# The opening of a forward convolution written anew: v and q mirrored on TensorE instead of in DRAM, the filter's fold in PSUM, SyncE's queue in program order

## The chip, the cores and the metric

One core of one Trainium2 chip. The time is that of one launch in microseconds (us), by the device's clock; the median of three runs stands for a kernel.

## The reference

A forward pass of four layers and its backward pass, for 2048 tokens of width 512 in bf16. The gradients of all inputs are outputs too. Only the first layer is touched here:

```python
x = A_q
x = x + _A_ref(_layernorm(x), A_k, A_v, A_shift_k, A_ssm_k, A_ssm_D)   # this layer
x = x + _B_ref(_layernorm(x), B_w1, B_b1, B_w2, B_b2)                  # MLP with gelu
...                                                                    # both once more, shared weights
# _A_ref(q, k, v, shift_k, ssm_k, ssm_D):
k_shift = sum over t < 4 of k_pad[:, t:t + S, :] * shift_k[:, 3 - t]   # a convolution of 4 taps
kv = k_shift * v
y = irfft(rfft(kv, 2 * S) * rfft(ssm_k, 2 * S))[:S]                    # a long convolution
y = y + kv * ssm_D
return q * y
```

## The kernel before

The long convolution is done with matrices. A sequence of 2048 is folded into blocks of 512 (`Fold`), one half of each block taken backwards, so that sums and differences (`fold_x`, then `fold_s` or `fold_d`, then `fold_t`) are multiplied with tables of cosines and sines on TensorE. The 4096-point spectrum is worked through in five groups of frequencies (`GROUPS`; 2, 2, 4, 4 and 4 blocks of 128). The same is done for the filter h (`A_ssm_k`, table `tabN`) and for kv (table `tabF`). `product` multiplies the two spectra per group on VectorE (DVE), `inv_group` transforms back on TensorE (PE), into `W`; `InvBlocks` unfolds on DVE.

Because of the fold, tokens of the second half of each 512 are kept in reversed order. The kernel before makes reversed copies in DRAM for that (`flip_rows`: `vB` of v, `qB` of q, `goB` of the output's gradient), and loads half a slice from the input and half from the copy (`tok_io`). A "slice" is 512 tokens: four slices of k, v, q.

The phase, `phase_conv_forward`, runs so:
- The filter is loaded as `hN`; per chunk of 128 channels PE transposes it (`ha_ps`, `hb_ps`), DVE and ScalarE (ACT) evict to `hA` and `hR`; PE reverses `hR` (`hr_ps` to `hB`), and DVE adds and subtracts (`fold_x<-hA,hB`). `sin_of` makes the tables: DVE computes angles (`tab_u`), ACT takes the sine.
- k is transposed per slice (`k_slice`: `kt_ps`, `kT`), and its convolution with 4 taps is done on PE with diagonal matrices (`ks_slice`: `ks_ps`, evicted by ACT to `ksb`). DVE multiplies with v (`y_res<-ksb,vt`: kv).
- `h_group` makes the filter's spectrum of a group on PE (`sp_ps`), ACT evicts it to `Hg`, and it is stored to `Hspec_d`. Between, PE turns tables (`table_turns`, `tt_ps`).
- kv is folded; `spectrum(g)` makes its spectrum (`KVg`, stored to `KVspec_d`), `load_spec(g)` loads `Hg` back, and then `product`, `inv_group`. q's four slices are normalised (`norm_sums`: statistics, POOL's rstd, `norm_apply`) and stored to `n_d`: slices 2 and 3 ahead of product 0, slices 0 and 1 between products 0 and 2.
- At the end: `x_sl`, the sum of q and the gated convolution, its statistics, and `l_n`, with which the MLP (`phase_mlp`) begins. The MLP first turns its weights on PE (`oo_ps`, evicted by ACT to `w1T_sb` and `w2T_sb`), and 11 one-column matmuls on `l_g` bring the bias b1 into columns.

What sets the order: in this phase the calls on PE and DVE keep the program's order (`Ordered`); the order on SyncE (SP), which issues most DMAs, is set by a scheduler. From the MLP on a planner sets the order; its rows on PE are the same in both kernels.

Of the kernel before, what the change touches and what calls it, by code (L numbers as in the profile page):

```python
# [177 lines left out]
def sin_of(nc, consts, pool, out, krow, pv, shift, np_=P, eng=None):  # L178
    n = krow.shape[-1]
    us = []  # L180
    for c0 in range(0, n, 1024):
        w = min(1024, n - c0)
        u = pool.tile([P, 1024], I32, name="tab_u", tag="tab_u", bufs=3)[0:np_, 0:w]
        (eng or (nc.vector if c0 else nc.gpsimd)).tensor_scalar(out=u, in0=krow[:, c0:c0 + w], scalar1=pv, scalar2=float(shift), op0=ALU.mult, op1=ALU.add)
        us.append((c0, w, u))
    for c0, w, u in reversed(us):
        nc.vector.tensor_single_scalar(out=u, in_=u, scalar=8191, op=ALU.bitwise_and)
        nc.scalar.activation(out=out[:, c0:c0 + w], in_=u, func=ACT.Sin, scale=SIN_SCALE, bias=consts.pibias[0:np_, :])
# [230 lines left out]
def phase_conv_forward(ctx, nc, tc, dims, consts, dram, res, aps):  # L419
# [80 lines left out]

    def ks_slice(i):
        vt = iop.tile([P, 4, D], BF16, name="vt", tag="vt", bufs=2)
        tok_io(nc, vt, v_ap, dram.vB, i)
# [10 lines left out]
        tt(out=kv[:, 4 * i:4 * i + 4, :], in0=ksb, in1=vt, op=ALU.mult)  # L514

    hA = foldp.tile([P, 4, 1024], BF16, name="hA", tag="fold_s", bufs=1)
    hB = foldp.tile([P, 4, 1024], BF16, name="hB", tag="fold_d", bufs=1)
    hR = foldp.tile([P, 4, 1024], BF16, name="hR", tag="fold_t", bufs=2)

    def h_chunk(cc):  # L520
        b = cc * S
        for m in range(2):
            c = slice(m * 512 + cc * P, m * 512 + (cc + 1) * P)
            ps = psum.tile([P, 4, P], F32, name="ha_ps", tag="kt", bufs=2)
            for i in range(4):
                nc.tensor.matmul(ps[:, i, :], lhsT=hN[:, b + 512 * i + m * P:b + 512 * i + m * P + P], rhs=consts.ident,
                                 start=True, stop=True)
            nc.vector.tensor_copy(out=hA[:, :, c], in_=ps)
            ps = psum.tile([P, 4, P], F32, name="hb_ps", tag="ks", bufs=2)
            for i in range(4):  # L530
                t0 = b + 512 * (i or 4) - m * P - P + 1
                nc.tensor.matmul(ps[:, i, :], lhsT=hN[:, t0:t0 + P], rhs=consts.ident, start=True, stop=True)
            nc.scalar.activation(out=hR[:, :, c], in_=ps, func=ACT.Identity)
        ps = psum.tile([4, P], F32, name="hs_ps", tag="kt", bufs=2)
        nc.tensor.matmul(ps, lhsT=hN[:, b + 256:b + S:512], rhs=consts.ident, start=True, stop=True)
        nc.vector.tensor_copy(out=hsp[0:4, cc * P:(cc + 1) * P], in_=ps)

    for cc in range(ND):
        qt, f = cc // 2, cc % 2
        sin_of(nc, consts, gp, tabN[:, f, qt, :], krow, pvn[:, qt:qt + 1], 2048 * (1 - f), eng=nc.vector)  # L540
        h_chunk(cc)
        if cc >= 2:
            k_slice(cc - 2)
    wshf = gp.tile([P, ND, 4], F32, name="wshf")
    nc.vector.tensor_copy(out=wshf, in_=wsh)
    for cc in range(ND):
        for j in range(4):
            nc.vector.tensor_scalar(out=wdiag[:, cc, j, :], in0=consts.ident, scalar1=wshf[:, cc, j:j + 1],
                                    scalar2=None, op0=ALU.mult)

    for m in range(2):
        for i in range(4):
            ps = psum.tile([P, 512], F32, name="hr_ps", tag="ks", bufs=2)
            nc.tensor.matmul(ps, lhsT=consts.anti, rhs=hR[:, i, m * 512:(m + 1) * 512], start=True, stop=True)
# [1324 lines left out]
```

## Time and profile before

| | |
|---|---|
| median of 3 runs | 848.1 us (847.89 to 851.46) |
| profiled execution | 852.29 us, its span 850.5 us |
| mean granted TensorE clock in it | 0.975 of full speed |
| busy: PE, DVE, ACT, POOL | 755.1, 738.5, 576.4, 207.0 us |

A busy time adds the time in which an engine worked on anything; what an engine waits for is seen in the timelines, which give each row's start, its length and, in brackets, the idle time ahead of it with what ended it.

### The profile page before, as it was taken

The numbers are of one execution on the slowest core, as the hardware profiler recorded it, in microseconds if no ns is written. First come the engines' busy times: TensorE is split into PE (matmuls) and PEld (weight loads), VectorE is DVE, ScalarE is ACT, GpSimd is POOL, SyncE is SP. The second block draws the span as 40 slices with busy tenths as digits, with TensorE's granted clock in tenths as the row PEclk, the third lists the DMA queues.
The fourth block names the chain that finished last, engine by engine and source line by source line (L and its number), as shares of the span: only waits on it lengthen the run. The fifth ranks groups of instructions, "written<-read, shape, count | busy, mean of one in ns | idle before, by whom it ended". The sixth has DMA issues, their size and how long they took to land.

```text
span 850.5 us, 13768 instructions
## 1 busy us (share of the span) xinstructions
PE 755.1 (89%) x5065; PEld 451.7 (53%) x5139; DVE 738.5 (87%) x1289; ACT 576.4 (68%) x818; POOL 207.0 (24%) x329
## 2 busy tenths in 40 slices
PE   4787878967988899999999999988999989999996
PEld 3463323445465566567565656633444446856763
DVE  9948479898999999999979998797399989999982
ACT  6867654668999899997779976445333228655662
POOL 5511210020325233333514213240110403400000
PEclk9999998998899899999999999999999999999998
DMA  6588866403644645746867486999699999793311
GB/s 231 206 323 319 290 229 241 156 9 105 185 143 139 165 133 148 210 146 200 201 193 182 135 249 154 292 207 283 185 280 247 200 385 322 249 319 98 106 62 37
DMA packets 203698, 169.40 MB, mean 199 GB/s; under 512 B 94379, under 2 KB 181614, under 8 KB 203374
## 3 DMA queue, kind: packets, MB, share of 16 engines
q1 hardware_dynamic: 187998, 122.07, 51.2%
q0 software_dynamic: 12400, 40.15, 14.0%
q10 hardware_dynamic: 3232, 6.29, 1.9%
q8 instruction: 40, 0.66, 0.3%
q14 instruction: 28, 0.23, 0.1%
HBM read 78.46 MB, written 76.36 MB: 182 GB/s over the span
## 4 chain that ended last, share of the span: by engine, by line
PE 40%; DVE 28%; ACT 17%; issue 6%; DMA 5%; POOL 3%; ACTq 0%; DVEq 0%; POOLq 0%
PE dw_ps L55 12%; ACT l_g L55 8%; DVE l_g L55 7%; PE sp_ps L55 7%; PE mm_ps L55 5%; PE oo_ps L55 5%; PE iv_ps L55 4%; DVE gy_bf L55 4%; PE gh_ps L55 3%; DVE l_h L55 2%; ACT l_n L55 2%; DVE b_junk L55 2%; DVE b1a L55 2%; DMA G<-n_d 2%; DVE ln_sts L55 1%
## 5 line engine op out<-in xcount | busy, mean ns | idle before, releaser
L55 ACT ACTIVATE l_g<-l_g 128x1536 bf16<-128x1536 bf16 (+1 forms) x96 | 134.9, 1439 | 1.0 <-DVE l_g L55 0.8
L55 PEld LDWEIGHTS <-l_h 128*128 128x128 bf16 x704 | 68.9, 98 | 87.5 <-DVE l_h L55 9.2
L55 PEld LDWEIGHTS <-dw_tm 128*128 128x128 bf16 x704 | 66.6, 98 | 74.2 <-issue 5.7
L55 PEld LDWEIGHTS <-w_sb 128*128 128x128 bf16 x836 | 80.3, 100 | 43.7 <-issue 21.9
L55 PE MATMUL mm_ps<-l_nT,w_sb 128*128 128x256 bf16 x704 | 92.4, 278 | 1.2 <-ACT l_g L55 0.4
L55 PE MATMUL oo_ps<-w_sb,l_h 128*128 128x512 bf16 x341 | 82.3, 386 | 7.6 <-DVE l_h L55 6.8
L55 PE MATMUL dw_ps<-G,dw_tm 128*128 128x512 bf16 x340 | 84.4, 382 | 4.2 <-DMA G<-n_d 3.5
L55 PE MATMUL dw_ps<-x_sl,dw_tm 128*128 128x512 bf16 x340 | 83.2, 379 | 1.7 <-ACT dw_tm L1584 1.1
L55 PE MATMUL mm_ps<-l_nT,w2T_sb 128*128 128x256 bf16 x704 | 82.9, 272 | 1.4 <-ACT l_h L55 0.9
L55 PE MATMUL oo_ps<-w1T_sb,l_h 128*128 128x512 bf16 x339 | 77.3, 379 | 1.8 <-DVE l_g L55 0.6
L55 DVE TENSOR_TENSOR l_g<-l_g,l_g 128x1280 bf16<-128x1280 bf16 (+1 forms) x88 | 76.5, 882 | 0.3
L55 PEld LDWEIGHTS <-w2T_sb 128*128 128x128 bf16 x704 | 68.8, 98 | 14.1 <-issue 2.1
L55 ACT ACTIVATE l_h<-mm_ps 128x512 bf16<-128x512 f32 (+1 forms) x96 | 52.1, 598 | 28.0 <-PE mm_ps L55 19.0
L1584 ACT ACTIVATE dw_tm<-dw_tp 128x1024 bf16<-128x1024 bf16 x44 | 44.7, 1024 | 34.5 <-PE dw_tp L55 27.6
L55 DVE TENSOR_REDUCE b1a<-dw_fm 128x1 f32<-128x2048 bf16 x22 | 49.8, 2279 | 3.2 <-DMA dw_fm<-gz_d 3.2
L55 POOL TENSOR_SCALAR l_dg<-ident,b_cols 128x128 bf16<-128x128 bf16 x32 | 31.7, 989 | 75.1 <-DVE b_junk L55 73.7
L55 ACT ACTIVATE l_n<-x_sl,nmr,rstd 128x512 bf16<-128x512 bf16 x48 | 38.2, 857 | 8.2 <-POOL nmr L989 4.6
L1646 ACT ACTIVATE dw_o<-dw_ps 128x512 bf16<-128x512 f32 x22 | 13.1, 597 | 40.2 <-PE dw_ps L55 30.6
L55 POOL TENSOR_SCALAR rstd<-ln_mvs 128x2 f32<-128x2 f32 x20 | 13.3, 664 | 110.1 <-DVE ln_mvs L55 110.0
L55 DVE TENSOR_SCALAR l_g<-l_g 128x1536 bf16<-128x1536 bf16 (+1 forms) x64 | 32.5, 519 | 3.5 <-ACT l_g L55 3.5
L55 ACT ACTIVATE l_g<-mm_ps,b_col 128x256 bf16<-128x256 f32 x77 | 32.9, 539 | 3.6 <-PE mm_ps L55 3.4
L55 PE MATMUL iv_ps<-Yg,tabI 128*128 128x512 bf16 x108 | 26.3, 395 | 8.5 <-DVE Yg L55 8.3
(293 smaller groups left out, 1599.0 us busy)
## 6 DMA issues: line engine op xcount, KB each, us to landing
h_d<-l_h SPq DMA_DIRECT2D x16, 704.0 KB, 4.6
gz_d<-l_h SPq DMA_DIRECT2D x16, 704.0 KB, 4.6
dw_fm<-gz_d SPq DMA_DIRECT2D x22, 512.0 KB, 9.4
l_n<-n_d SPq DMA_DIRECT2D x28, 256.0 KB, 4.7
n_d<-l_n SPq DMA_DIRECT2D x24, 256.0 KB, 2.9
Hspec_d<-Hg ACTq DMA_DIRECT2D x8, 512.0 KB, 3.0
Hg<-Hspec_d SPq DMA_DIRECT2D x3, 1024.0 KB
KVspec_d<-KVg SPq DMA_DIRECT2D x3, 1024.0 KB, 5.2
```

Of the source, the lines that this page charges most:

```text
L55: return self.tc.keep_in_program_order(f(*args, **kwargs))
L1584: nc.scalar.activation(out=dst, in_=ps, func=ACT.Identity)
L1646: nc.scalar.activation(out=o, in_=ps, func=ACT.Identity)
```

## The change

- The tiles of the MLP's weights are allocated first (`weight_tiles`), and serve as landing places for h and then for q. `start_weights` loads the weights themselves after product 0.
- The filter's fold: `h_back` transposes the reversed part to `hR`; `h_both` adds, in PSUM, the transposed chunk and `hR` through a signed, reversed identity (`turn`), for sum and difference at once (`hx_ps`); one eviction per step goes straight to `fold_x`, in turn by ACT and DVE.
- v is loaded in whole slices; PE mirrors two of its four blocks (`vr_ps`), and DVE reads them from PSUM in the product. q is loaded once; PE mirrors it (`q_turn`, `qr_ps`), ACT evicts, POOL stores `qB`. All four slices of q are normalised ahead of product 0, and two of them loaded back from `n_d` into `y_res`.
- `tabN` is built in halves, the second ones after group 1; `h_group(2)` comes ahead of `ks_slice(3)`.
- `vB` and `goB` are made late, after the last KVspec store and ahead of the MLP's first loads.
- SP keeps the program's order too.

The core of the diff (unchanged parts and small rearrangements left out):

```diff
-    nc = Ordered(nc, tc, ("tensor", "vector"))
+    nc = Ordered(nc, tc, ("tensor", "vector", "sync"))
...
-    flip_rows(nc, dram.vB, v_ap, 511)
-    flip_rows(nc, dram.qB, aps["A_q"].flatten_outer_dims(), 511)
...
+    def kv_slice(i):
+        tt(out=kv[:, 4 * i:4 * i + 2, :], in0=ksbs[i][:, 0:2, :], in1=vts[i][:, 0:2, :], op=ALU.mult)
+        for h in (2, 3):
+            ps = psum.tile([P, D], F32, name="vr_ps", tag="kt", bufs=2)
+            nc.tensor.matmul(ps, lhsT=consts.anti, rhs=vts[i][:, 5 - h, :], start=True, stop=True)
+            tt(out=kv[:, 4 * i + h, :], in0=ksbs[i][:, h, :], in1=ps, op=ALU.mult)
...
+    def h_both(cc, m):
+        t, b = hat[cc]
+        ps = psum.tile([P, 2, 4, P], F32, name="hx_ps", tag="sp", bufs=2)
+        for sg in range(2):
             for i in range(4):
+                t0 = b + 512 * i + m * P
+                nc.tensor.matmul(ps[:, sg, i, :], lhsT=t[:, t0:t0 + P], rhs=consts.ident, start=True, stop=False)
+                nc.tensor.matmul(ps[:, sg, i, :], lhsT=turn[:, m, sg, :], rhs=hR[:, 2 * cc + m, i, :], start=False, stop=True)
+        out = hX[:, :, :, m * 512 + cc * P:m * 512 + (cc + 1) * P]
+        if m:
+            nc.scalar.activation(out=out, in_=ps, func=ACT.Identity)
+        else:
+            nc.vector.tensor_copy(out=out, in_=ps)
...
-    for i in range(4):
-        ks_slice(i)
-        if i < 2:
-            h_group(i)
-        if i in (1, 3):
-            sth.append(fh.streams(GROUPS[(i + 3) // 2][0]))
-        tabF_part(i)
+    for s in range(4):
+        nc.sync.dma_start(out=qs[s], in_=tok(aps["A_q"].flatten_outer_dims(), s))
+    k_slice(0)
+    k_slice(1)
+    ks_slice(0)
+    h_group(0)
+    kv_slice(0)
+    load_v(2)
+    k_slice(2)
+    k_slice(3)
+    ks_slice(1)
+    kv_slice(1)
+    load_v(3)
+    h_group(1)
...
+    ks_slice(2)
+    kv_slice(2)
+    sth.append(fh.streams(GROUPS[3][0]))
+    h_group(2, 2)
+    ks_slice(3)
+    kv_slice(3)
...
+    norm_sums(0)
+    h_group(3, 4)
+    norm_sums(1)
+    tabF_part(2)
+    norm_apply(0)
+    norm_apply(1)
+    tabF_part(3)
...
+    sts = [fk.streams(GROUPS[0][0])]
+    norm_sums(2)
+    norm_sums(3)
+    norm_apply(2)
+    norm_apply(3)
...
+    for s in range(2):
+        nc.sync.dma_start(out=ns[s], in_=tok(dram.n[0], s))
...
         if g == 0:
-            norm_sums(0)
-            norm_sums(1)
-            res.w = start_weights(nc, wpool, dims, aps)
-        if g == 1:
-            norm_apply(0)
-            norm_apply(1)
+            start_weights(nc, res.w, dims, aps)
...
+    flip_rows(dram.goB, aps["grad_out"].flatten_outer_dims(), 511, nc.sync)
+    flip_rows(dram.vB, v_ap, 511, nc.sync)
```

Three places in the order of instructions. First DVE behind product 1 (`pr_t`, `pr_u` and `Yg` are a product's steps; `Hg_1307` and `Hg_1457` are the filter's group 1 in the two kernels, `Hg_1496` and `Hg_1547` its group 2). Before:

```order
L55 TENSOR_TENSOR Yg<-pr_u 128x1024
L55 TENSOR_SCALAR fold_s<-fold_d 128x2x1024
L55 TENSOR_SCALAR fold_s<-fold_s 128x1024 x2
L55 TENSOR_TENSOR fold_t<-fold_x,fold_s 128x1024 x2
L55 TENSOR_TENSOR fold_t<-fold_s,fold_x 128x1024 x2
L55 TENSOR_SCALAR y_res<-y_res,rstd_97,ln_nmr 128x512 x8
L55 TENSOR_TENSOR pr_t<-KVg,Hg_1496 128x2048
```

and in the changed kernel:

```order
L55 TENSOR_TENSOR Yg<-pr_u 128x1024
L55 TENSOR_SCALAR fold_s<-fold_d 128x2x1024
L55 TENSOR_SCALAR fold_s<-fold_s 128x1024 x2
L55 TENSOR_TENSOR fold_t<-fold_x,fold_s 128x1024 x2
L55 TENSOR_TENSOR fold_t<-fold_s,fold_x 128x1024 x2
L55 TENSOR_TENSOR pr_t<-KVg,Hg_1547 128x2048
```

The eight applications (`y_res<-y_res,rstd`) ahead of product 2 are gone, as are eight pairs of statistics between products 0 and 1; both now stand before `fold_x` of kv.

Second, SP's queue from group 0's KVspec store to the load of the filter's group 2. Before:

```order
L663 DMA KVspec_d<-KVg 256x1x1024
L246 DMA y_res<-in_A_q_dram 128x2x512
L652 DMA n_d<-y_res 128x4x512
L246 DMA y_res<-qB_d 128x2x512
L652 DMA n_d<-y_res 128x4x512
L246 DMA y_res<-in_A_q_dram 128x2x512
L246 DMA y_res<-qB_d 128x2x512
L657 DMA Hg_1496<-Hspec_d 128x2x2048
```

and in the changed kernel (two `n_d` stores of 128x4x512 and the load of group 1's `Hg`, 128x2x1024, stand right ahead of it):

```order
L55 DMA KVspec_d<-KVg 256x1x1024
L55 DMA y_res<-n_d 128x4x512 x2
L55 DMA w_sb<-in_B_w_dram 128x4x1376
L55 DMA w_sb<-in_B_w_dram 128x10x512
L55 DMA w_sb<-in_B_w_dram 96x512
L55 DMA w_sb<-in_B_b_dram 1x512
L55 DMA KVspec_d<-KVg 256x1x1024
L55 DMA Hg_1547<-Hspec_d 128x2x2048
```

The weights (`w_sb<-in_B_w_dram`), which stood far ahead, behind the loads of v, now stand between group 0's KVspec store and the load of the filter's group 2.

Third, SP's queue at the end of the phase. Before, the last KVspec store is followed at once by the loads of b1 (`l_g<-in_B_b_dram`):

```order
L663 DMA KVspec_d<-KVg 256x1x2048
L55 DMA l_g<-in_B_b_dram 1x4x128
L55 DMA l_g<-in_B_b_dram 1x128
```

and in the changed kernel:

```order
L55 DMA KVspec_d<-KVg 256x1x2048
L55 DMA goB_d<-in_grad_out_dram 1024x1x512
L55 DMA vB_d<-in_A_v_dram 1024x1x512
L55 DMA l_g<-in_B_b_dram 1x4x128
L55 DMA l_g<-in_B_b_dram 1x128
```

Two reversed copies of 1 MB now stand between them; `goB` stood behind the weights before, `vB` at the very start, next to `qB`, which is no longer copied in DRAM.

## Rows read from the trace of the kernel before

**Rows 1.** Timeline of PE, 0 to 66 us: start, length, instruction, idle time before it.
```profile
4.34 0.61 PE L55 MATMUL ha_ps<-ident,hN 128*128 128x128 bf16 x4 [4.34 <-DMA hN<-in_A_ssm_k_dram]
...
39.03 0.38 PE L55 MATMUL sp_ps<-fold_t,tabN 128*128 128x512 bf16 x1 [0.53 <-DVE fold_t L55]
...
56.44 3.73 PE L55 MATMUL ks_ps<-wdiag,kT 128*128 128x128 bf16 x64 [1.10 <-ACT ksb L512]
60.01 0.38 PE L55 MATMUL sp_ps<-fold_d,tabN 128*128 128x512 bf16 x1
...
65.14 1.07 PE L55 MATMUL tt_ps<-ident,tabN 128*128 128x128 bf16 x16
69.31 0.61 PE L55 MATMUL tt_ps<-ident,tabN 128*128 128x128 bf16 x8 [3.10 <-ACT tg L202]
```

**Rows 2.** Timeline of DVE, 9 to 67 us.
```profile
9.20 1.28 DVE L55 CAST hA<-ha_ps 128x512 bf16<-128x512 f32 x2
...
30.90 4.49 DVE L55 TENSOR_TENSOR fold_x<-hA,hB 128x4096 bf16<-128x4096 bf16 x2
35.43 2.29 DVE L55 TENSOR_TENSOR fold_s<-fold_x 128x4096 bf16<-128x4096 bf16 x1
37.75 2.36 DVE L55 TENSOR_TENSOR fold_t<-fold_s 128x2048 bf16<-128x2048 bf16 x2
...
41.52 1.50 DVE L55 TENSOR_SCALAR tab_u<-krow,pvh 128x1024 int32<-128x1024 f32 x2
43.05 1.29 DVE L55 TENSOR_SCALAR tab_u<-tab_u 128x1024 int32<-128x1024 int32 x2
...
62.01 0.16 DVE L55 CAST tabF<-alt 128x1 bf16<-128x1 f32 x1 [5.04 <-ACT tabF L188]
...
65.94 1.22 DVE L55 TENSOR_TENSOR y_res<-ksb,vt 128x2048 bf16<-128x2048 bf16 x1
```

**Rows 3.** Timeline of DVE, 94 to 137 us.
```profile
94.20 1.23 DVE L55 TENSOR_TENSOR fold_t<-fold_s 128x2048 bf16<-128x2048 bf16 x1 [9.11 <-PE sp_ps L55]
...
102.13 1.39 DVE L55 TENSOR_SCALAR y_res<-y_res,rstd,ln_nmr 128x512 bf16<-128x512 bf16 x4 [0.33 <-POOL ln_nmr L989]
...
111.92 1.23 DVE L55 TENSOR_TENSOR pr_t<-KVg,Hg 128x2048 bf16<-128x2048 bf16 x1 [1.77 <-ACT KVg L323]
...
118.27 0.69 DVE L55 BATCH_NORM_STATS2 ln_st<-y_res 128x6 f32<-128x512 bf16 x1
...
125.73 0.47 DVE L55 MEMSET w_sb<- 128x64 uint32 x2
...
133.94 2.67 DVE L55 TENSOR_SCALAR y_res<-y_res,rstd,ln_nmr 128x512 bf16<-128x512 bf16 x8
136.52 1.21 DVE L55 TENSOR_TENSOR pr_t<-KVg,Hg 128x2048 bf16<-128x2048 bf16 x1
```

**Rows 4.** Timeline of SP's queue, 9 to 160 us.
```profile
9.86 0.80 SPq L231 DMA_DIRECT2D vB_d<-in_A_v_dram  x1
...
20.49 12.62 SPq L246 DMA_DIRECT2D vt<-in_A_v_dram  x1
...
157.77 0.52 SPq L663 DMA_DIRECT2D KVspec_d<-KVg  x1
```

**Rows 5.** Table by stretch: length, busy time of PE, PEld, DVE, ACT, POOL, clock, DMA share, GB/s.
```profile
4.00:8.00 4.00, 2.07 (x16) 1.63 (x17) 3.43 (x11) 1.37 (x3) 4.00 (x18) 1.00 1.00 365
...
120.00:124.00 4.00, 4.00 (x20) 1.78 (x19) 2.96 (x8) 2.48 (x3) 1.70 (x4) 1.00 0.97 302
```

**Rows 6.** Timeline of PE, 143 to 178 us.
```profile
143.14 6.63 PE L55 MATMUL iv_ps<-Yg,tabI 128*128 128x512 bf16 x29 [1.70 <-DVE Yg L55]
...
156.52 14.06 PE L55 MATMUL iv_ps<-Yg,tabI 128*128 128x512 bf16 x62
...
177.17 0.42 PE L55 MATMUL oo_ps<-l_g 128*128 128x1 bf16 x11
```

**Rows 7.** Timeline of ACT, from 183 us.
```profile
187.71 2.93 ACT L55 ACTIVATE l_n<-x_sl,nmr,rstd 128x512 bf16<-128x512 bf16 x4 [4.55 <-POOL nmr L989]
```

More of the change, by code (lines that the diff above doesn't have):

```diff
@@ L170, in build_consts @@
         nc.vector.memset(c.pibias, math.pi * (1.0 - SIN_EPS))
+        c.zero = const_pool.tile([P, 1], F32, name="zero")
+        nc.scalar.activation(out=c.zero, in_=c.onescol_f, func=ACT.Sin, scale=0.0)
     return c
@@ L175, with sin_of @@
 SIN_SCALE = -(2.0 * math.pi / 8192.0) * (1.0 - SIN_EPS)
[L178 to L188, printed above, removed]
+def sin_of(nc, consts, pool, out, krow, pv, shift):
+    u = pool.tile([P, 1024], I32, name="tab_u", tag="tab_u", bufs=3)
+    nc.vector.tensor_scalar(out=u, in0=krow, scalar1=pv, scalar2=float(shift), op0=ALU.mult, op1=ALU.add)
+    nc.vector.tensor_single_scalar(out=u, in_=u, scalar=8191, op=ALU.bitwise_and)
+    nc.scalar.activation(out=out(), in_=u, func=ACT.Sin, scale=SIN_SCALE, bias=consts.pibias)
 def table_turns(nc, psum, pool, consts, tabN, dramG, tabF, tabI, dramI):
@@ L207, in table_turns @@
     tgs = {}
-    for f in range(2):
-        for k0 in (0, 8):
+    for k0 in (0, 8):
+        for f in range(2):
             for qt in range(2):
@@ L513, in ks_slice @@
         nc.gpsimd.dma_start(out=dram.ks[:, 4 * i:4 * i + 4, :], in_=ksb)
[L514 to L524, printed above, removed]
-            for i in range(4):
[L526 to L536, printed above, removed]
@@ L538, in phase_conv_forward @@
-    for cc in range(ND):
[L539 to L554, printed above, removed]
-            nc.scalar.activation(out=hB[:, i, m * 512:(m + 1) * 512], in_=ps, func=ACT.Identity)
-    for i in range(2, 4):
-        k_slice(i)
-    krow5 = gp.tile([P, 1024], F32, name="krow5", tag="tab_u", bufs=3)[0:5, 0:5 * P]
-    for gi, (k1, base, n) in enumerate(GROUPS):
-        nc.vector.tensor_copy(out=krow5[:, gi * P:(gi + 1) * P], in_=krow[0:5, base * P:(base + 1) * P])
@@ new lines, in phase_conv_forward, with h_back @@
+    hX = res.xpool.tile([P, 2, 4, 1024], BF16, name="fold_x", tag="fold_x", bufs=1)
+    hR = foldp.tile([P, 8, 4, P], BF16, name="hR", tag="fold_d", bufs=1)
+    def h_back(cc, m):
+        t, b = hat[cc]
+        ps = psum.tile([P, 4, P], F32, name="hb_ps", tag="ks", bufs=2)
+        for i in range(4):
+            t0 = b + 512 * (i or 4) - m * P - P + 1
+            nc.tensor.matmul(ps[:, i, :], lhsT=t[:, t0:t0 + P], rhs=consts.ident, start=True, stop=True)
+        nc.scalar.activation(out=hR[:, 2 * cc + m], in_=ps, func=ACT.Identity)
@@ new lines, in phase_conv_forward @@
+    ps = psum.tile([4, D], F32, name="hs_ps", tag="kt", bufs=2)
+    for cc in range(ND):
+        t, b = hat[cc]
+        nc.tensor.matmul(ps[:, cc * P:(cc + 1) * P], lhsT=t[:, b + 256:b + S:512], rhs=consts.ident, start=True, stop=True)
+    nc.vector.tensor_copy(out=hsp[0:4, :], in_=ps)
+    for f, u in enumerate((sp5u, krow5)):
+        nc.vector.tensor_single_scalar(out=u, in_=u, scalar=8191, op=ALU.bitwise_and)
+        nc.scalar.activation(out=sp5[:, f, :], in_=u, func=ACT.Sin, scale=SIN_SCALE, bias=consts.pibias[0:5, :])
@@ L682, in phase_conv_forward @@
             load_spec(g)
+        if g == 4:
+            res.x = res.xpool.tile([P, NT, D], BF16, name="x_sl", tag="fold_x", bufs=1)
+            for s in range(4):
+                tok_io(nc, res.x[:, s * TS:(s + 1) * TS, :], aps["A_q"].flatten_outer_dims(), dram.qB, s)
         H = Hs[g]
```

216 lines of the change are left out of this document (124 added, 92 removed).

## The prediction, made before the changed kernel was run

> **What bounds the kernel now.** I read the page's busy times first, in the table above: PE is busy 755.1 us of 850.5, DVE 738.5. Neither share says much here, because all edits lie in the forward convolution, before the MLP, and everything from the MLP on is the same work in the same order. So the change is worth the shift of the MLP's start, and I measure that on ACT's first `l_n` (187.71 us, [rows 7]). I then read the start backwards along the timelines.
>
> PE ends the phase with an unbroken run: from Yg's second half of group 2 (143.14) it goes through the last inverse transforms until 170.4 [rows 6]. What lets it start is DVE's product 2 at 136.52, behind product 0 at 111.92 [rows 3]. Between the two DVE has no idle time to speak of: normalising q's first half (statistics 118.27 to 125.73, application 2.67) stands in that stretch. Before product 0 it is PE that holds DVE: the longest wait is 9.11 us, until PE has read the old `fold_t` for the filter's spectrum [rows 3]. In the opening the first spectrum matmul comes at 39.03 [rows 1], behind the filter's fold on DVE (30.90 to 40.1, [rows 2]).
>
> **Part 1, the filter's opening: 13 us earlier.** Removed: the `fold_x` pair of 4.49, the hA casts (8 of 0.64), the reversal through `hr_ps`/`hB`, the krow casts. Added: 8 steps, each 4 + 16 matmuls of 128 columns and an eviction of 1024 from PSUM. A matmul takes 0.0575 us at 56.44 (64 in 3.73) and about 0.105 in the first rows (4 in 0.61, of which some 0.2 is the tail that the next one overlaps) [rows 1]; the granted clock reads 1.00 there too [rows 5], so the rows give two paces and not the reason. A step is then 2.1 us by PE at the slow pace, or 1.35 by DVE's half of the work (a cast of 1024, twice 0.64, and a half table, (1.50 + 1.29)/2, every second step [rows 2]). Eight steps from about 5.5 us (the second part of h) end at 16.5 to 22.5; fold_s 2.3 and fold_t 2.4 follow [rows 2], and waits of about 2. First spectrum matmul at 23 to 29; I take 26, the middle, since the trace gives no rule for when the pace changes. PE has k's first transposes and ks(0) between, 5.6 to 8 by the prices below, which ends at about the same time. 13 us gained.
>
> **Part 2, the gain is spent on PE before the fourth kv product.** PE's new order from there: group 0's 13 matmuls, mirrors, k's transposes of slices 2 and 3, ks(1), group 1, ks(2), then group 2 (40) with 32 turns, and only then ks(3). Prices by [rows 1]: ks 3.73 each, three times, plus up to 0.8 each for evictions; 20 spectrum matmuls 5.13 (60.01 to 65.14), so 10.3 for group 2 and 6.4 for the 25 of groups 0 and 1; 32 transposes of k 1.9 to 3.4 by the two paces; 32 turns 2.1 to 4 (16 in 1.07, then waits for ACT's copies, one of them 3.10); mirrors about 1.3. Sum 33 to 39. I take 38, near the end with the waits, which the rows show on turns. Slice 3's product starts near 64 (56 to 68). Before it was issued at 65.94 [rows 2], so part 1 is gone here: DVE waits for PE in the meantime.
>
> **Part 3, DVE from there to product 0: 3 us later than before.** Its queue, each price a row [rows 2, 3]: kv(3) 1.9; group 4's fold_t 2.4 (as much as the two of 2048); eight half tables 11.2 and two casts 0.3; statistics of q's slices 0 and 1, 6.4 (95.3 to 102.1 less the wait of 0.33); application 2.7; fold_x 4.5; fold_s 2.3; fold_t 1.2; statistics of slices 2 and 3, 6.4; application 2.7 and POOL's waits before it 1; fold_t 1.2. Sum 44.2. On top come four small rows on `Hg` and waits for ACT's sines, of which one was 5.04 [rows 2]; I take 6.8 in all (1 to 10). Product 0 starts at 64 + 44.2 + 6.8 = 115 (109 to 121), against 111.92. No row shows a product with a PSUM operand; I bound its 128x512 by 0.30 (a quarter of one fold_t of 2048 from SBUF, half of 2.36) and 0.64 (the cast from PSUM), and take the upper, because it reads the same source. The Trainium skill (VectorE: DVE Perf Modes, The perf-mode tier table) puts tensor_tensor with any PSUM operand at 1x, 2293 ns for 2048 elements, by which the sum would be 0.1 us lower; no row here shows it.
>
> **Part 4, product 0 to product 2: DVE 10 us shorter.** 24.60 before; less 7.46 and 2.67 leaves 14.4. DVE could start product 2 at 129.4, 7.1 us earlier than before.
>
> **Part 5, the load of H[2] takes most of it back.** Product 2 also needs `Hg` for group 2. Before, its load was issued right behind product 0 and the weights had long been loaded. Now the same queue of SP holds, from the store of normalised slice 2 on (about 111: ahead of product 0 stand half an application, 1.4, fold_t 1.2 and the small rows): two n_d stores 1.05 MB, H[1] 0.52, KVspec 0.52, two n_d loads 1.05, weights 2.82, KVspec 0.52, H[2] 1.05: 7.5 MB. DMA moved 365 GB/s at 4 to 8 us and 302 at 120 to 124, both at full or nearly full share [rows 5]; 340, between them, gives 22.2 us, the bounds 20.6 and 25. With 1 us to land, an estimate: 134.2 (132 to 137). So product 2 waits for its load and starts 2.3 us earlier than before (5 earlier to 1 later). Behind H[2] waits nothing else on SP that DVE needs sooner; behind product 2 on DVE stand all later products. The Trainium skill (DMA: Bandwidth & Descriptors, Two DMAs through the same engine are not ordered) says that descriptors of one queue of one engine start in order, which speaks against this placement; the trace agrees where 256 KB of v, issued behind the two mirrored copies, left SP only after 12.62 us [rows 4]. Were the load free to pass the weights, 1 MB at 340 from its issue near 124 would be there by 128, and DVE's 129.4 would decide.
>
> **Part 6, the flips ahead of b1.** PE's run of 27 us after product 2 is unchanged [rows 6], so x_sl and `l_n`'s inputs are 2.3 earlier. But SP now issues goB and vB, two row-reversed copies of 1 MB, right before the b1 loads. Two such copies held SP from 9.86 to 33.1 [rows 4]. From the last KVspec store (about 155.5): 155.5 + 23.3 + 1.7 (my estimate for issuing and landing) = 180.5 for b1, which PE's 11 columns want at 177.17 - 2.3 = 174.9. PE stalls 5.6, and the evictions behind it on ACT stand ahead of `l_n`: from the columns to the last of them 183.16 - 177.17 = 6 [rows 6, 7], so `l_n` not before 186.5, and about 186.7 instead of 185.4. That costs 1.3 (0 where the copies take under 22 us, up to 4 at 26).
>
> **Costed at nothing:** mirroring q on PE (8 matmuls, 4 evictions, in PE's time before DVE arrives), w-diagonal, POOL's shorter copies, one table load less: DVE or PE is the later one each time. If that cover went, q's four evictions of about 1 us would show first.
>
> **Sum.** -2.3 + 1.3 = -1.0 us at `l_n`. The profiled execution took 852.29 us (span 850.5), 4.2 above the median of the runs, 848.1: 851.3 there, 847.1 for the median. A change under about 0.5% (4.2 us) can't be told from none here.
>
> **Rivals.**
> (a) *Faster, about 842.* Product 0 comes at 113 and the queue drains at 365 GB/s: 109 + 20.6 + 1 = 130.6, 6 earlier than before, and the flips cost nothing. It decides from product 2 at 132.3 on (4.2 earlier). For: 365 at 4 to 8 us. Against: 302 at 120 to 124, where stores and loads are mixed as here [rows 5]. The same comes out if H[2] needn't queue behind the weights.
> (b) *Slower, about 853.5.* The opening stays at the slow pace and ACT's waits are large: kv(3) at 68, product 0 at 68 + 44.2 + 9 = 121.2, the queue from 117.4, H[2] at 140.6, 4.1 later than before, and the flips' 1.3. It decides from product 0 at 120 on. For: the first rows show the slow pace. Against: at that pace a step is 2.1 us, which alone moves the product to 67 only.
> (c) *Slower by the flips alone, about 854.* They share the DMA engines with x_sl's loads and last 30 us: b1 at 187.5, `l_n` at 193.5. Decides from 29 us on; two copies in 23.3 speak against it.
> (d) *Nothing moves.* PE or DVE is bound as before at product 2: that is within the forecast.
>
> **How the numbers follow.** Forecast (within 0.5%) 0.42; (a) 0.33; (b) 0.16; (c) 0.09. So faster 0.33, same 0.42, slower 0.25. The forecast's own range is 843 to 851 (H[2] from 132 to 137, flips 0 to 4). With (a) down to 839 and (b) up to 857 about 0.8 is held.
>
> **What would show it.** Right: first spectrum matmul near 26; DVE waiting on PE or ksb before the fourth product near 64; product 0 near 115; DVE waiting on the DMA of `Hg` before product 2, near 134; PE stalled for the `l_g` load near 175 to 180; `l_n` near 186.7. Wrong: product 0 later than 120 or earlier than 111, H[2] in place when DVE arrives, or b1 in time; or a difference behind `l_n`, which the sum takes as none.

## The result and the profile after

Against runs of the kernel before beside it, the change took 854.47 us (median of 9; 851.38 to 858.64) where before took 848.01 (9; 846.98 to 851.46): the ratio is 1.0072, with a 95% interval of 1.0052 to 1.0092. That is slower, by about 6 us. The profiled execution took 855.12 us, its span 853.2, where before's took 852.29 and 850.5. The first `l_n` starts at 193.60 instead of 187.71, which is 5.9 us later.

The page of the changed kernel, busy time by engine:

```profile
span 853.2 us, 14021 instructions
## 1 busy us (share of the span) xinstructions
PE 766.9 (90%) x5243; PEld 456.7 (54%) x5243; DVE 733.2 (86%) x1257; ACT 578.5 (68%) x822; POOL 200.1 (23%) x321
```

PE is busy 11.8 us more than before and DVE 5.3 less, and neither tells where the end went. So read the places where the prediction put its marks. The timeline of DVE after (start, length, instruction, idle time before it and what ended it):

```profile
26.82 2.36 DVE L55 TENSOR_TENSOR fold_t<-fold_s 128x2048 bf16<-128x2048 bf16 x2
...
64.57 0.69 DVE L55 TENSOR_TENSOR y_res<-ksb,vt 128x1024 bf16<-128x1024 bf16 x1 [8.87 <-ACT ksb L540]
...
115.35 1.22 DVE L55 TENSOR_TENSOR pr_t<-KVg,Hg 128x2048 bf16<-128x2048 bf16 x1
...
135.16 1.23 DVE L55 TENSOR_TENSOR pr_t<-KVg,Hg 128x2048 bf16<-128x2048 bf16 x1 [5.12 <-DMA Hg<-Hspec_d]
...
178.87 1.22 DVE L55 TENSOR_TENSOR x_sl<-y_res,x_sl 128x2048 bf16<-128x2048 bf16 x1
```

The filter's `fold_t` is 11 us earlier than in [rows 2]. On PE the first spectrum matmul follows it, 10.7 us earlier than in [rows 1]:

```profile
28.33 0.59 PE L55 MATMUL sp_ps<-fold_t,tabN 128*128 128x512 bf16 x2
```

Then the wait of 8.87 ahead of the fourth kv product takes the gain. Product 0 is 3.4 later than in [rows 3], product 2 only 1.4 earlier, with a new wait of 5.12 for the filter's load. Now SP's queue (start, time that the instruction held the queue):

```profile
117.45 6.37 SPq L55 DMA_DIRECT2D w_sb<-in_B_w_dram  x3
...
124.84 0.62 SPq L55 DMA_DIRECT2D Hg<-Hspec_d  x1
...
158.10 0.52 SPq L55 DMA_DIRECT2D KVspec_d<-KVg  x1
158.67 0.79 SPq L55 DMA_DIRECT2D goB_d<-in_grad_out_dram  x1
159.50 9.66 SPq L55 DMA_DIRECT2D vB_d<-in_A_v_dram  x1
172.66 9.52 SPq L55 DMA_DIRECT2D l_g<-in_B_b_dram  x5
```

The load of H[2] (the filter's group 2, `Hg`) is issued at 124.84, behind the weights and one KVspec store. At the end b1's loads are issued at 172.66 and can't be handed over until 182.18. PE's timeline shows who waits for them:

```profile
141.78 8.32 PE L55 MATMUL iv_ps<-Yg,tabI 128*128 128x512 bf16 x30 [2.94 <-DVE Yg L55]
...
186.07 0.43 PE L55 MATMUL oo_ps<-l_g 128*128 128x1 bf16 x11 [8.40 <-DMA l_g<-in_B_b_dram]
186.36 1.87 PE L55 MATMUL oo_ps<-w_centre,w_sb 128*128 128x512 bf16 x4
...
188.45 1.91 PE L55 MATMUL oo_ps<-w_centre,w_sb 128*128 128x512 bf16 x4
...
190.58 1.05 PE L55 MATMUL oo_ps<-w_centre,w_sb 128*128 128x512 bf16 x4
```

The 11 columns come 8.9 us later than in [rows 6], after a stall of 8.40. The first two groups of four matmuls behind it take 1.87 and 1.91 instead of the 1.05 of the third: PE is granted a slower clock after it stood. The table by stretch has that clock and what the DMA engines did (columns as in [rows 5]):

```profile
140.00:148.00 8.00, 6.22 (x22) 2.48 (x21) 7.94 (x13) 2.11 (x3) 0.00 (x0) 0.79 0.95 329
...
172.00:176.00 4.00, 3.92 (x28) 2.10 (x27) 3.93 (x6) 3.90 (x12) 0.00 (x0) 1.00 0.27 97
...
180.00:184.00 4.00, 0.00 (x0) 0.00 (x0) 3.83 (x10) 0.00 (x0) 0.49 (x1) 0.55 0.27 97
184.00:188.00 4.00, 1.93 (x15) 0.88 (x16) 3.90 (x7) 0.18 (x1) 3.75 (x4) 0.50 0.07 24
188.00:192.00 4.00, 4.00 (x23) 2.29 (x22) 3.90 (x6) 1.30 (x3) 0.01 (x1) 0.67 0.00 0
```

From 172 to 184 the two mirrored copies are nearly alone: 97 GB/s at a share of 0.27, against 302 and 365 in [rows 5]. A share of 0.27 means that the 16 DMA engines were idle for most of that time, so it is not other traffic that makes the copies slow. The DMA view says what ran on SP's queue (its packets, MB and share), first from 158 to 163 us, then from 163 to 186, and the table by stretch when it ended:

```profile
q1 hardware_dynamic: 268, 1.05, 58.5%
...
q1 hardware_dynamic: 2082, 2.10, 25.7%
...
185.00:186.00 1.00, 0.00 (x0) 0.00 (x0) 0.96 (x3) 0.00 (x0) 1.00 (x1) 0.50 0.02 7
```

So the 1 MB KVspec store, issued at 158.10, comes first. The copies' 2.10 MB move from 163 to about 185, and the columns follow at 186.07.

PE's clock reads 0.55, 0.50 and 0.67 from 180 to 192, around the stall (0.50 is the 1.2 GHz level), and also 0.79 at 140 to 148, behind the wait of 2.94. Last, ACT's timeline, which ends the chain:

```profile
186.53 0.18 ACT L55 ACTIVATE b_col<-oo_ps 128x11 f32<-128x11 f32 x1 [8.23 <-PE oo_ps L55]
...
192.98 0.60 ACT L55 ACTIVATE w1T_sb<-oo_ps 128x512 bf16<-128x512 f32 x1 [0.49 <-PE oo_ps L55]
193.60 2.93 ACT L55 ACTIVATE l_n<-x_sl,nmr,rstd 128x512 bf16<-128x512 bf16 x4
```

`l_n` has no wait before it any more. In [rows 7] it waited 4.55 for `nmr`, which POOL makes from the statistics and `rstd`; now it stands behind the evictions that stand behind the columns.

### The profile page after: what moved, and what is told of

Read it like the earlier page. It is cut to its first block, busy times and chain, and to the rows that moved or that the text cites. A ratio compares the mean times of both kernels' runs of the same rounds, so it can differ in the third digit from the quotient of the medians.

```text
span 853.2 us, 14021 instructions
## 1 busy us (share of the span) xinstructions
PE 766.9 (90%) x5243; PEld 456.7 (54%) x5243; DVE 733.2 (86%) x1257; ACT 578.5 (68%) x822; POOL 200.1 (23%) x321
## 4 chain that ended last, share of the span: by engine, by line
PE 46%; DVE 24%; ACT 19%; issue 5%; DMA 2%; POOL 2%; SPq 0%; ACTq 0%; DVEq 0%; POOLq 0%
PE dw_ps L55 15%; ACT l_g L55 9%; PE sp_ps L55 7%; DVE l_g L55 6%; PE oo_ps L55 6%; PE iv_ps L55 5%; PE mm_ps L55 5%; DVE gy_bf L55 4%; PE gh_ps L55 3%; ACT l_n L55 3%; DVE l_h L55 2%; DVE b1a L55 2%; PE dw_tp L55 2%; DVE b_junk L55 2%; DVE ln_sts L55 1%
## 5 line engine op out<-in xcount | busy, mean ns | idle before, releaser
L55 PEld LDWEIGHTS <-w_sb 128*128 128x128 bf16 x936 | 90.1, 102 | 45.4 <-issue 19.9
L55 PE MATMUL dw_ps<-G,dw_tm 128*128 128x512 bf16 x352 | 87.1, 387 | 3.6 <-ACT dw_tm L1641 3.6
L55 PE MATMUL dw_ps<-x_sl,dw_tm 128*128 128x512 bf16 x352 | 85.3, 379 | 2.2 <-ACT dw_tm L1641 2.2
L55 PE MATMUL oo_ps<-w1T_sb,l_h 128*128 128x512 bf16 x352 | 79.1, 379 | 1.0 <-DVE l_g L55 0.6
L1641 ACT ACTIVATE dw_tm<-dw_tp 128x1024 bf16<-128x1024 bf16 x44 | 44.6, 1024 | 36.2 <-PE dw_tp L55 21.7
L55 ACT ACTIVATE l_n<-l_n,b_cols 128x512 bf16<-128x512 bf16 x32 | 25.5, 847 | 10.2 <-POOL b_cols L55 10.1
```

Of the source, the lines that this page charges most:

```text
L55: return self.tc.keep_in_program_order(f(*args, **kwargs))
L1641: nc.scalar.activation(out=dst, in_=ps, func=ACT.Identity)
```

## The experiments

Theory: the loss is the two mirrored copies ahead of b1, by their length alone; H[2]'s place behind the weights is a second, smaller wait. Rival: the reordered opening (PE's order up to the fourth kv product) costs the time, and the late b1 only covers it. All of the experiments start from the changed kernel. A table of all of them stands at the end of this section.

**1 to 4, places on SP's queue.** `e1_flips_early` issues the copies behind the loads of v:

```diff
@@ behind the loads of v's last slice
+    flip_rows(dram.goB, aps["grad_out"].flatten_outer_dims(), 511, nc.sync)
+    flip_rows(dram.vB, v_ap, 511, nc.sync)
@@ conv_forward, behind the loop over groups
-    flip_rows(dram.goB, aps["grad_out"].flatten_outer_dims(), 511, nc.sync)
-    flip_rows(dram.vB, v_ap, 511, nc.sync)
```

> The changed kernel with its two reversed copies (goB, vB) issued on SP right behind the load of v's slice 3, at about 40 us, where SP issues nothing until 88, and not ahead of the b1 loads. Theory (the copies ahead of b1 cost the time): PE's 11 columns come at about 177.6 as in the kernel before, l_n at about 188.0 instead of 193.6, time 854.5 - 5.6 = 848.9. Rival 1 (the loss lies in the redesigned opening, and the stall only hides slack): l_n stays within 1 us of 193 and the time at 853 or more. Rival 2 (the copies only move their price, since they now run beside the loads and stores of 40 to 64 us): kv(3) or product 0 comes 3 us or more later than 64.6 and 115.4, time 851 to 853.

Ratio 1.0017 [0.9993, 1.0041], no difference that can be told. The columns come at 177.40 with no wait, and `l_n` at 187.94. So with the copies gone from there, the loss at `l_n` is gone too (193.60 to 187.94). But in this build the loads of H[0] also moved behind the last stores of normalised q, as SP's queue shows:

```profile
39.54 1.31 SPq L55 DMA_DIRECT2D goB_d<-in_grad_out_dram  x1
...
87.80 25.33 SPq L55 DMA_DIRECT2D n_d<-w_sb  x4
113.31 1.41 SPq L55 DMA_DIRECT2D Hg<-Hspec_d  x2
```

Product 0 waits 5.13 for H[0] and starts at 120.17. That costs nothing at product 2 (136.03), which no longer waits for H[2]: one wait took the other's place.

`e2_filter_first` leaves the copies and loads H[2] ahead of the weights:

```diff
@@ ahead of the loop over groups
-    for s in range(2):
-        nc.sync.dma_start(out=ns[s], in_=tok(dram.n[0], s))
@@ in the loop
-        if g >= 2:
+        if g >= 3:
             load_spec(g)
...
         if g == 0:
+            load_spec(2)
+            for s in range(2):
+                nc.sync.dma_start(out=ns[s], in_=tok(dram.n[0], s))
             start_weights(nc, res.w, dims, aps)
```

> The changed kernel with the load of the filter's group 2 ahead of the n_d loads and the weights on SP; the copies stay ahead of b1. Theory (product 2 waits for a load that queues behind the weights, and the copies then hold b1): product 2 at 130.0 instead of 135.2, KVspec(4) and the copies 5 us earlier, b1's columns at 181 instead of 186, l_n at 188.4, time about 849.3. Rival (the wait for Hg is covered, another limit is right behind it): product 2 or the last inverse transform moves by less than 2 us, time 853 or more.

Ratio 1.0053 [1.003, 1.0076]. Product 2 starts at 129.48 with no wait, but only 2.5 of these 5.7 us reach `x_sl` (176.33). ACT's timeline shows why:

```profile
135.97 1.94 ACT L317 ACTIVATE KVg<-sp_ps 128x1024 bf16<-128x1024 f32 x2 [4.55 <-DMA KVspec_d<-KVg]
```

The eviction of group 3's spectrum needs the buffer of group 1's, whose store stands behind the weights as well. The columns wait 8.42 for b1, at 183.55. From the copies' issue to the columns it is 27.43 us (156.12 to 183.55), in the changed kernel 27.40 (158.67 to 186.07): the KVspec store right ahead and the two copies set this time, whenever they start.

`e3_both` has both edits, as they stand above:

> Both edits. Theory (two queue positions on SP, each worth its own time): product 2 at 130, columns of b1 without a wait, l_n at about 183, time 843.8, 4 us faster than the kernel before. Rival (the two stalls cover each other, so the second edit adds little): time 848 to 849, as with one of them.

Ratio 1.0042 [1.0021, 1.0064]; product 0 119.81, product 2 134.41, columns 179.38 without a wait, `l_n` 189.91. I expected the gains to add. They didn't: product 0 is late again, by H[0], and now product 2 is late with it, 4.9 behind e2's.

`e4_third_flip` copies `goB` a third time at the same place, a doubling of the suspected cost:

```diff
     flip_rows(dram.vB, v_ap, 511, nc.sync)
+    flip_rows(dram.goB, aps["grad_out"].flatten_outer_dims(), 511, nc.sync)
```

> The changed kernel with a third reversed copy (goB once more) behind the two, ahead of b1. Theory: b1 comes later by the length of one copy, 10.8 to 13 us, and so does the MLP: time 865 to 868. Rival (the stall at b1 is covered by other waits): 855 to 859.

Ratio 1.0198 [1.0149, 1.0248]. PE's timeline:

```profile
196.64 0.43 PE L55 MATMUL oo_ps<-l_g 128*128 128x1 bf16 x11 [19.26 <-DMA l_g<-in_B_b_dram]
```

That is 10.57 us later than with two copies, and `l_n` is 10.24 later (203.84). A copy of 1 MB costs its whole 10.6 us here, just under the 10.8 to 13 expected, so the theory's mechanism stands, and its size nearly.

**5, 6 and 8, another queue.** `e5_flips_pool` issues both copies from POOL's queue, in the idle stretch behind the last table store:

```diff
+    late = Ordered(nc, tc, ("gpsimd",))
+    turns = table_turns(late, psum, gp, consts, tabNs, dram.tabG, tabF, tabI, dram.tabI)
...
-    flip_rows(dram.goB, aps["grad_out"].flatten_outer_dims(), 511, nc.sync)
-    flip_rows(dram.vB, v_ap, 511, nc.sync)
+    flip_rows(dram.goB, aps["grad_out"].flatten_outer_dims(), 511, late.gpsimd)
+    flip_rows(dram.vB, v_ap, 511, late.gpsimd)
```

> The changed kernel with goB and vB copied from POOL's queue, behind the last tabI store (about 107 us), so that no load of SP stands behind them. Theory: b1's columns come without a wait, at about 177.5, and l_n at 188, time 5.6 below the changed kernel's, about 848.9 against 848.0 of before. Rival (two copies in another queue take the engines from SP's loads all the same): Hg for group 2 lands 4 us or more later than 135, and l_n at 191 or later.

Ratio 1.0152 [1.0134, 1.0169], worse than the change. b1 is in time, but DVE waits three times. Its timeline:

```profile
112.77 1.38 DVE L55 TENSOR_SCALAR w_sb<-w_sb,rstd,nmr 128x512 bf16<-128x512 bf16 x4 [3.57 <-POOL nmr L1047]
...
131.86 1.23 DVE L55 TENSOR_TENSOR pr_t<-KVg,Hg 128x2048 bf16<-128x2048 bf16 x1 [6.16 <-DMA Hg<-Hspec_d]
...
147.59 1.23 DVE L55 TENSOR_TENSOR pr_t<-KVg,Hg 128x2048 bf16<-128x2048 bf16 x1 [8.41 <-DMA Hg<-Hspec_d]
```

The first wait is the order on POOL: issuing the copies takes it 1.72 and 1.69, between the steps that make `rstd` and `nmr`, and product 0 starts at 118.17 instead of 115.35. Product 1 waits where the copies run beside its load. The Trainium skill (DMA: Bandwidth & Descriptors, Issuing engines are not separate DMA queues) says that DMAs of different issuing engines end on the same 16 DMA engines and interleave; this wait agrees. Product 2's load was issued only at 137.75, 12.9 later than in the change and after the copies had landed (124.4 and 129.7): the queue ahead of it was late by then.

`e6_weights_late` adds e2's order to e5 and puts `start_weights` behind the loads of `x_sl`:

```diff
@@ in the loop, group 4, behind the loads of x_sl
+            start_weights(nc, res.w, dims, aps)
@@ in the loop, group 0
-            start_weights(nc, res.w, dims, aps)
-        if g == 2:
-            res.w.finish()
+            load_spec(2)
...
@@ behind the loop
+    res.w.finish()
```

> As e5, and the load of the filter's group 2 right behind product 0, the weights only behind the loads of x_sl (about 145 us), so that neither Hg nor the KVspec stores, which free KVg for ACT, stand behind them. Theory: product 2 at 130, no wait of ACT for a KVspec store at 132 to 136, the run of inverse transforms 5 us earlier, l_n at about 183, time 843.8. Rival (the wait is passed on once more, to a transfer that I don't see, or PE's slower clock takes it): l_n at 186 or later.

Ratio 1.0099 [1.0073, 1.0125]: product 1 still waits 7.29 for its filter and `l_n` is at 193.34. The weights, now far behind it, were not what H[1] waited for.

`e8_kv_first` is e6 with the fourth kv product's `ks` ahead of the filter's group 2 on PE, the test of the rival (the opening's order):

```diff
@@ ahead of ks(3) and the fourth product
-    h_group(2, 2)
@@ behind them
+    h_group(2, 2)
-    sth.append(fh.streams(GROUPS[4][0]))
@@ behind the next half table
+    sth.append(fh.streams(GROUPS[4][0]))
```

> As e6, and on PE ks(3) and the fourth kv product ahead of the filter's group 2, with group 4's fold moved behind the statistics of slice 1 so that DVE needn't wait for PE there. Theory (the 10 us that the opening gains are spent in DVE's wait for ks(3)): fourth product at about 54 instead of 64.6, product 0 near 109, product 2 near 124.5, l_n near 178, time about 838. Rival (PE's total of spectra and turns bounds product 0, since fold_t of group 1 waits for the filter's last group): product 0 at 112 or later, time above 841.

Ratio 1.01 [1.0072, 1.0127], the same as e6. The fourth product is early, but DVE then waits 11.58 and 5.48 for ACT's sines of `tabF` (at 74.18 and 96.74) and product 0 comes at 119.85. So undoing the opening's order on PE doesn't bring the time back. What was expected of PE's total isn't shown either: what holds DVE here is ACT.

**7, 9 and 10.** `e7_forward_copy` has two copies of the same bytes with ascending rows (it leaves out the mirroring, so the gradients that use them are not the reference's):

```diff
-        ap=[[512 * rs, out.shape[0]], [-rs, n], [1, src2d.shape[1]]]))
+        ap=[[512 * rs, out.shape[0]], [rs, n], [1, src2d.shape[1]]]))
...
-    flip_rows(dram.goB, aps["grad_out"].flatten_outer_dims(), 511, nc.sync)
+    flip_rows(dram.goB, aps["grad_out"].flatten_outer_dims(), 256, nc.sync)
```

> The changed kernel with the two copies at the same place and of the same bytes, but rows in ascending order, so that goB and vB aren't mirrored (the gradients that use them are left wrong; the time alone is read). Theory (what stands ahead of b1 costs its own length, and the reversed rows make it long): ascending rows run at the 350 to 420 GB/s of other transfers, about 6 us for both, b1 lands before 170, columns at about 177.5, l_n at 188, time about 848.9. Rival (any copy from DRAM to DRAM runs at 97 GB/s, or the stall isn't the copies'): columns at 183 or later, time above 852.

Ratio 1.0056 [1.0031, 1.0081]: between theory and rival. The copies hold SP for only 1.28 instead of 9.66, yet its table by stretch has them at only 135 and 131 GB/s:

```profile
164.00:168.00 4.00, 4.00 (x20) 1.79 (x19) 3.93 (x5) 2.17 (x4) 0.00 (x0) 1.00 0.32 135
168.00:172.00 4.00, 3.95 (x25) 2.08 (x25) 3.93 (x5) 3.03 (x7) 0.00 (x0) 1.00 0.30 131
```

The columns still wait 5.71, 24.7 us from the issue instead of 27.4. So reversal accounts for a part; these copies from DRAM to DRAM are slow here either way.

`e9_flips_before_kvspec` puts the same two lines behind the loads of `x_sl`, ahead of the last KVspec store:

```diff
@@ in the loop, group 4, behind the loads of x_sl
+            flip_rows(dram.goB, aps["grad_out"].flatten_outer_dims(), 511, nc.sync)
+            flip_rows(dram.vB, v_ap, 511, nc.sync)
@@ behind the loop
-    flip_rows(dram.goB, aps["grad_out"].flatten_outer_dims(), 511, nc.sync)
-    flip_rows(dram.vB, v_ap, 511, nc.sync)
```

> The changed kernel with goB and vB right behind the loads of x_sl (about 149 us), ahead of the last KVspec store and not behind it. Theory: the copies run from 152 to 174 beside PE's last run, the KVspec store 3 us, b1 lands at about 178: columns at 178, l_n at 188 to 189, time about 849.5. Rival (the copies hold what the phase itself still needs there): the last inverse transform or x_sl later by 2 us or more, time 852 or more.

Ratio 1.0025 [1.0002, 1.0048], two thirds of the loss recovered. The columns come at 183.24, without a wait for b1. The wait has moved to that store, for which ACT now waits:

```profile
178.74 2.06 ACT L55 ACTIVATE w1T_sb<-oo_ps 128x512 bf16<-128x512 f32 x4 [4.04 <-DMA KVspec_d<-KVg]
```

`e10_release_queue` orders the queue by when things are needed: H[2] right behind product 0, the weights behind H[3], the copies from POOL's queue when product 3 is done (a `mark` that reads its result):

```diff
-        if g >= 2:
+        if g >= 3:
             load_spec(g)
+        if g == 3:
+            start_weights(nc, res.w, dims, aps)
...
         if g == 0:
+            load_spec(2)
...
+        if g == 3:
+            late = Ordered(nc, tc, ("gpsimd",))
+            mark = invp.tile([P, 1], BF16, name="mark")
+            late.gpsimd.tensor_copy(out=mark, in_=Ys[3][1][:, 1, 0, 0:1])
+            flip_rows(dram.goB, aps["grad_out"].flatten_outer_dims(), 511, late.gpsimd)
+            flip_rows(dram.vB, v_ap, 511, late.gpsimd)
...
```

> The changed kernel with three positions changed: the filter's group 2 is loaded right behind product 0; the weights stand behind the load of the filter's group 3 and not ahead of both; goB and vB go from POOL's queue when product 3 is done (about 148 us), so that b1 isn't behind them. Theory (each wait on SP's queue was its own): product 2 at 130, no ACT wait for a KVspec store of group 1, l_n at about 183, time about 843.8. Rival (DMA as a whole is the bound from 111 to 177 us, about 15 MB of loads and stores and 22 us of reversed copies, so the wait moves to H[4], x_sl or b1): l_n at 186 or later, time above 846.5.

Ratio 1.0144 [1.0104, 1.0184], far off. Yet `x_sl` is at 173.52, 5.0 ahead of before, and the columns at 171.90. POOL's timeline has the reason:

```profile
178.16 1.10 POOL L1046 TENSOR_SCALAR rstd<-ln_mv 128x4 f32<-128x4 f32 x1 [28.24 <-DVE ln_mv L55]
195.56 0.31 POOL L1046 TENSOR_SCALAR rstd<-ln_mv 128x4 f32<-128x4 f32 x1 [16.30 <-DVE ln_mv L55]
195.84 2.18 POOL L1047 TENSOR_TENSOR rstd<-rstd,mhalf 128x4 f32<-128x4 f32 x2
```

In this build the steps of slices 0 and 1 are paired on POOL, so slice 0's `rstd` stood behind slice 1's statistics (until 195.5). This is the order of one queue, and no cost of a copy.

**11.** `e11_pool_order` is e10 with POOL's steps of the two slices in the program's order:

```diff
+    pool_order = Ordered(nc, tc, ("gpsimd",))
...
-        res.ln1[s] = norm_stats(nc, invp, res.mhalf, x, ...
+        res.ln1[s] = norm_stats(pool_order, invp, res.mhalf, x, ...
```

> The queue of the run before (H[2]'s load right behind product 0, the weights behind H[3], both mirrored copies from POOL's queue when product 3 is done), with one thing more: POOL's steps on the statistics of the first MLP's slices keep the order of the program, slice 0 ahead of slice 1. That run had the sum x_sl at 173.5, 5.0 us ahead of before, and the matmul columns at 171.9 with no wait, but its first l_n only at 198.7, because POOL's queue held slice 0's rstd (179.3) behind slice 1's statistics (195.6). Theory (the change's loss is where the copies stand, and H[2]'s place costs the rest of the gain): x_sl 173.5, nmr 9.1 us behind it as in the changed kernel (178.87 to 188.01), so l_n at 182.7 against 187.71 before, and the time about 5 us under before: ratio 0.994, 842 us. Rival (the opening has no gain to give, the MLP behind it waits for something else, such as the copies that then run until about 168, or slices 1 to 3, which were not moved as much): l_n at 182.7 but the time within 0.3% of before, and the 5 us reappear as a wait behind l_n, before 260 us.

843.45 us (12 runs) against 846.52 (17): ratio 0.9952 [0.9933, 0.997]. This version is faster than both kernels. ACT's timeline has `l_n` waiting for POOL again, as before the change:

```profile
182.64 2.93 ACT L55 ACTIVATE l_n<-x_sl,nmr,rstd 128x512 bf16<-128x512 bf16 x4 [4.73 <-POOL nmr L55]
```

The timeline of POOL's queue has the issue of the copies:

```profile
146.50 1.73 POOL L55 DMA_DIRECT2D goB_d<-in_grad_out_dram  x1
148.24 1.65 POOL L55 DMA_DIRECT2D vB_d<-in_A_v_dram  x1
```

and the view of DMA issues (the last number is us from issue to landing) when they landed, 165.4 and 170.4:

```profile
goB_d<-in_grad_out_dram POOLq DMA_DIRECT2D x1, 1024.0 KB, 18.9
vB_d<-in_A_v_dram POOLq DMA_DIRECT2D x1, 1024.0 KB, 22.2
```

The table by stretch shows what they ran beside:

```profile
152.00:156.00 4.00, 3.95 (x20) 1.78 (x19) 4.00 (x6) 2.35 (x4) 0.00 (x0) 1.00 1.28 285
156.00:160.00 4.00, 4.00 (x20) 1.79 (x19) 4.00 (x7) 2.18 (x4) 0.00 (x0) 1.00 1.09 364
```

A load is late here too, as DVE's timeline shows at product 4:

```profile
151.75 1.23 DVE L55 TENSOR_TENSOR pr_t<-KVg,Hg 128x2048 bf16<-128x2048 bf16 x1 [5.56 <-DMA Hg<-Hspec_d]
...
173.47 1.23 DVE L55 TENSOR_TENSOR x_sl<-y_res,x_sl 128x2048 bf16<-128x2048 bf16 x1
```

That wait is not the copies' doing. The DMA view has SP's queue alone from 140 to 151 (first line), and POOL's queue (q0), on which the copies were issued, only later (second line, from 152 to 160):

```profile
q1 hardware_dynamic: 2567, 4.20, 105.7%
...
q0 software_dynamic: 1458, 0.96, 49.0%
```

The load of the filter's group 4 was issued at 139.90, behind the 2.8 MB of weights that were issued from 130.69 on, and the DMA engines were full. The wait of 5.56 is covered: PE runs from 129.38 to 169.4 without a stop, since products 2 and 3 came early, and its clock stays at 1.00. `l_n` comes at 182.64, as expected, 5.1 ahead of [rows 7]. So the changed opening does have 5 us to give, and it was the order on the queues that kept them. The rival falls: the same opening is in the fastest kernel. No run gives the kernel before the same late queue, so how much of the 5 us is the opening's own is not separated.

All runs beside each other. The shift of `l_n` is that of the profiled execution against 187.71; the shift in time is the ratio less 1, times the median of before beside it:

| kernel | `l_n`, us | shift of `l_n` | ratio | shift in time |
|---|---|---|---|---|
| the change | 193.60 | +5.9 | 1.0072 | +6.1 |
| e1, copies behind v's loads | 187.94 | +0.2 | 1.0017 | +1.4 |
| e2, H[2] first | 190.29 | +2.6 | 1.0053 | +4.5 |
| e3, both | 189.91 | +2.2 | 1.0042 | +3.6 |
| e4, a third copy | 203.84 | +16.1 | 1.0198 | +16.8 |
| e5, copies on POOL at 109 | 198.80 | +11.1 | 1.0152 | +12.9 |
| e6, and weights late | 193.34 | +5.6 | 1.0099 | +8.4 |
| e8, and kv first | 195.39 | +7.7 | 1.01 | +8.5 |
| e7, ascending copies | 190.58 | +2.9 | 1.0056 | +4.7 |
| e9, copies ahead of KVspec | 189.26 | +1.6 | 1.0025 | +2.1 |
| e10, by release | 198.74 | +11.0 | 1.0144 | +12.2 |
| e11, and POOL's order | 182.64 | -5.1 | 0.9952 | -4.1 |

The time follows `l_n` in every row, and is 0.2 to 2.8 us more. The intervals are mostly about 2 us to either side, and all shifts of `l_n` are against one profiled execution of before, so whether there is a cost of about 1 us behind `l_n` stays open.

## Why the prediction was wrong

The forecast was "no change that can be told", -1.0 us; measured is +6.1. Rival (c), slower by the copies alone, with 0.09, has the numbers: b1 at 187.5 and `l_n` at 193.5 by it, 186.07 and 193.60 measured. Its reason is not what happened. The copies were to share the DMA engines with the loads of `x_sl`; these were issued until 148.75, and from 157 to 159 the engines were idle. That its numbers came so near is in part luck.

**The step that failed is Part 6, the copies ahead of b1**, priced at 1.3 us. By its own terms, against 186.7 for `l_n` and 193.60 measured:
- The last KVspec store was to come at 155.5, 2.3 ahead of before, and the copies with it. The copies were issued at 158.67: 3.2 late, because the gain of Part 5 didn't get that far.
- Copies and landing were to take 25.0 us (23.3, the time that two copies held SP in [rows 4], and 1.7). From issue to columns it was 27.4: 4 to 5 us behind the KVspec store, 22 of copies, and 1 until the columns. Ahead of the copies the sum had nothing. The 1.7 is an estimate for which no row stands; the 1 is the nearest that the runs show.
- From columns to `l_n` 6.2 was assumed, 7.5 measured, as PE ran at the slower clock after the stall. That is 1.3 us which the sum didn't have.

Together 3.2 + 2.4 + 1.3 = 6.9, the whole miss at `l_n`. The mechanism was named rightly (stall of PE at the columns, evictions ahead of `l_n`), but each of its three terms came out too early or too short. The 23.3, which is also the argument against rival (c), is a wrong reading of [rows 4]: it is the time until SP was free, not until the copies had landed. The trace of before has the copies' pace, and the first load of v behind them, issued at 20.49, with 18.6 us to its landing:

```profile
16.00:20.00 4.00, 2.42 (x24) 2.05 (x22) 3.96 (x8) 3.61 (x5) 0.00 (x0) 1.00 0.27 97
...
vt<-in_A_v_dram SPq DMA_DIRECT2D x1, 256.0 KB, 18.6
```

So that load was there at 39.1, 29.2 us after the first copy's issue at 9.86, and two copies of 1.05 MB at 97 GB/s are 21.6 us, to which comes whatever stands ahead of them.

**Part 5** had product 2 at 134.2, measured 135.16: -1.4 instead of -2.3 against before. e2 shows that H[2]'s load held it: with the load first it starts at 129.48, which is also Part 4's 129.4. The 1.4 was then lost: the inverse transforms of group 2 took 8.32 us instead of 6.63, at a granted clock of 0.79 in that stretch, 1.7 us that the prediction had as "unchanged". `x_sl` came 0.3 later than before instead of 2.3 earlier.

**Parts 1 to 4 held**: first spectrum matmul 28.33 (26, of 23 to 29), fourth kv product 64.57 behind a wait (64), product 0 at 115.35 (115). That the 64 is so near is in part luck: Part 1 came 2.3 later than taken, and PE's stretch of Part 2 was 36.2 instead of 38. The marks to watch were right but for the size of the last two: PE stood for `l_g` until 186.07, and `l_n` came at 193.60.

What the experiments add: e11 shows 5 us of gain, more than the forecast thought, as soon as H[2], the weights and the copies stand where what waits for them is covered. Rival (a)'s remark ("if H[2] needn't queue behind the weights") is half of that; e2 shows that alone it is not enough, since KVspec's store and b1 then wait in its place.

## What to carry to other kernels

When a change moves a transfer on a queue, write down what is behind it there, small loads included, and what is ahead of it. Take for its length the time until something behind it has landed, not the time for which the queue was held. A gain at the start of a phase counts only at the phase's end: here 11 us at the first fold had become 0.3 us late at `x_sl`, and moving three things on two queues, with POOL's order kept, brought 5 of them back. After each such move read the order of every engine again. Three times an order that nobody meant to change took away what was tried: H[0] behind the stores in e3, the copies' issue between POOL's steps in e5, POOL's statistics in e10.
